# Fewer matmuls of ones at the start of an attention and gMLP kernel, and its first score tiles in the order of their loads

## The chip, the cores and the metric

The kernel runs on one core of one Trainium2 chip. The metric is device time in microseconds (us). Before the change three runs gave a median of 536.39 us (536.26 to 537.36).

The core has five engines that matter here: PE (TensorE, matmuls; its weight loads are listed as PEld), DVE (VectorE), ACT (ScalarE), POOL (GpSimd) and SP (SyncE, which issues the DMAs). Each runs its own list of instructions in order and waits for the others through semaphores.

## The reference

What is computed, for a batch of 8, 8 heads, 576 positions and a head dimension of 64:

```python
# sliding-window attention with a distance bias
scores = scale * np.matmul(q, k.transpose(0, 1, 3, 2))      # scale = 1/8
bias   = slopes[:, None, None] * (-np.abs(rel))             # rel = query position - key position
mask   = (rel >= 0) & (rel < 128)
scores = np.where(mask, scores + bias, -1e9)
attn   = softmax(scores)                                    # row max off, exp, divided by sum + 1e-9
x      = (attn @ v) as [batch, 576, 512]

# gated MLP with a spatial product
h      = np.maximum(x @ w_in, 0)                            # 512 -> 1024
u, v   = h[..., :512], h[..., 512:]
v_n    = (v - mean(v)) / sqrt(var(v) + 1e-6)
v_s    = einsum('ts,bsd->btd', w_spatial, v_n) + b_spatial
out    = (u * v_s) @ w_out
```

## The kernel before

**Work.** Eight batch entries go through the same chain: scores, softmax, the product with v, then units of the gated MLP called v, u, s (spatial) and o (output). Entry 0 is done in another way from entries 1 to 7. Its matmuls run on f32 operands, because the weights split into f16 halves aren't ready yet. It is cut into tiles: tile `tT P` is 128 query positions (two blocks of 64) of head pair P, for T = 0 to 4 and P = 0 to 3. Tile 0 needs only the first 128 columns of q and k; tile 1 needs columns 0 to 255.

**A tile of entry 0**, in the names of the code and of the rows below:
- `raw_tile` (letter t): PE writes two score blocks into two of four PSUM buffers s0 to s3 (L696). DVE adds the bias table, and takes the row extreme (L705). ACT takes the exponential, with the row sum (L709). Block widths are 64 and 128 columns for tile 0 and 192 for the others.
- `raw_sums` (letter m), once for each T: DVE adds 1e-9 and takes the reciprocal (L717, L718) once the four pairs of that tile row have their sums.
- `raw_out` (letter n): DVE or ACT scales the blocks (L730, L731), PE transposes them (L738, `ident`), DVE or ACT copies the transposed blocks to `pq` (L412), PE multiplies with v (L753), and DVE or ACT copies the result to `xt` (L412).

Beside these tiles DVE and ACT turn the weights, which arrive as 64-bit words, into f32 (`bits64`, L430 to L449, five steps over 128x512 for each of twelve pieces), and scale and split them.

**What sets the order.** Every piece of work is recorded in a `Plan` with its engine, an assumed weight in ns, a due time and the buffers that it reads and writes. Where `either` is used, the piece may go to ACT or to DVE. The string `OPENING` gives the order in which the opening's pieces are recorded, which fixes the turns on rotating buffers. `Plan.emit` then simulates the engines forward and backward up to 12 times on the assumed weights, takes the order whose simulated end is earliest, and writes each engine's list in that order. So a change in the string, or in one weight, reorders all engines. In that simulation PE's weights count double before `COLD`, and the DMAs cost more before `SLOW`.

**Matmuls of ones.** `constants` records `WARM` matmuls of a 128x256 block of ones into a PSUM buffer that nobody reads (L395). They depend only on the memsets, and the plan places them where it thinks that PE is free. `emit` has a second such device: where the plan shows PE idle for more than `SPARE` = 400 ns between `SLOW` = 9000 and `UNTIL` = 95000 ns of simulated time, it puts matmuls of ones of 128x128 into half of the rest of that gap (`filler`). In the kernel before, no gap calls for one.

**Loads.** SP issues the DMAs in the order of the plan. For entry 0 each head pair's q and k come in three pieces: 128, 256 and 192 columns (128, 256 and 192 KB).

Of the kernel before, what the change touches and what calls it, by code (L numbers as in the profile page):

```python
# [55 lines left out]
class Plan:  # L56
# [3 lines left out]

    PASSES, COLD, SLOW = 12, 6000, 9000
    LAG = {"PE": 200, "DVE": 130, "ACT": 130, "POOL": 150, "SP": 2200}

    def __init__(self):
# [125 lines left out]
                self.filler(int((idle - self.SPARE) * self.FILL / self.filler_ns))  # L192
            self.ops[n][0][best[2][n]][2]()

    SPARE, FILL, UNTIL = 400, 0.5, 95000

    def idle(self, out, way, ended, begun):

        last = None
        for n in out:  # L200
            gap = 0
            if self.ops[n][0][way[n]][0] == "PE":
                if last is not None and self.SLOW < begun[n] < self.UNTIL and begun[n] - ended[last] > self.SPARE:
                    gap = begun[n] - ended[last]
                last = n
            yield n, gap
# [3 lines left out]
def attn_gmlp_kernel(ctx, tc, qk, v, w_in, w_spT, b_sp, w_out, outT):  # L210
# [3 lines left out]
    nc = tc.nc  # L214
# [14 lines left out]
    NB = S // D  # L229

    SWITCH = 190
    SCORES, VALUES, BOTH = 1600, 1800, 2760


    WX = 12
    OPENING = (
# [8 lines left out]
    )  # L245
    UORDER = {B - 1: "uuuuusussusussssoooooooo"}
    USUAL = "uuuuusussususoooosssoooo"
# [32 lines left out]
    def pe(*cols):  # L280
        return sum(12 + n / 2.38 for n in cols)
# [114 lines left out]
            plan.add("PE", pe(2 * P), 0, f, [(ones, 0), (fill, 0)])  # L396

    SLOTS = 7
    WARM = 64
    NM_, SM_, TM_, RC_ = range(4)  # L400
    RSTAT = [(rstat, (i, k, c)) for i in range(2) for k in range(4) for c in range(2 * NP)]

# [280 lines left out]
    def raw_tile(p, t, k, raw, due):  # L683

        blocks = [i for i in (2 * t, 2 * t + 1) if i < NB]
        sc = [plan.buf(ps, "s", 4, [P, 512], F32) for _ in range(2)]
        flat = lambda e: sc[e]().rearrange("p a b -> p (a b)")
        st = lambda kind, e: rstat()[:, t % 2, kind, e * NP + p:e * NP + p + 1]
        key = lambda kind, e: (rstat, (t % 2, kind, e * NP + p))

        def f():
            for e, i in enumerate(blocks):
                n = min(i + 1, 3) * D
                for j in range(2):
                    q = slice((j ^ e) * D, ((j ^ e) + 1) * D)
                    nc.tensor.matmul(flat(e)[q, :n], raw()[j * D:(j + 1) * D, 0, i * D:(i + 1) * D],  # L696
                                     raw()[j * D:(j + 1) * D, 1, (i + 1) * D - n:(i + 1) * D], start=True, stop=True, skip_group_check=True)
        plan.add("PE", SWITCH + pe(4 * W), due, f, [(raw, x) for x in range(max(0, t - 1), t + 1)], [(x, 0) for x in sc])
        for e, i in enumerate(blocks):
            n = min(i + 1, 3) * D  # L700
            pr = lambda e=e, n=n: slot_ap(k)[:, W - n:W] if e == 0 else slot_ap(k)[:, 512 - n:]
            cols = slot_parts(k, e)

            def f(e=e, n=n, pr=pr):
                nc.vector.tensor_tensor_reduce(pr(), flat(e)[:, :n], tabs()[:, 2 * p + e, W - n:], -0.125, 3e38, ALU.add, ALU.min, st(NM_, e))  # L705
            plan.add("DVE", dve(n), due + 300, f, [(sc[e], 0), (tabs, 2 * p + e)], cols + [key(NM_, e)])

            def f(e=e, pr=pr):
                nc.scalar.activation(pr(), pr(), AF.Exp, bias=st(NM_, e), scale=-1.0, accum_out=st(SM_, e))  # L709
            plan.add("ACT", act(n, 2), due + 600, f, cols + [key(NM_, e)], cols + [key(SM_, e)])  # L710
# [10 lines left out]
    def raw_out(p, t, k, vr, xt, due):  # L721
# [2 lines left out]
        tiles = [x for x in (t - 1, t) if x >= 0]  # L724
        st = lambda e: rstat()[:, t % 2, RC_, e * NP + p:e * NP + p + 1]
        cols = [x for e in range(len(blocks)) for x in slot_parts(k, e)]
        for e, i in enumerate(blocks):
            n = min(i + 1, 3) * D
            pr = lambda e=e, n=n: slot_ap(k)[:, W - n:W] if e == 0 else slot_ap(k)[:, 512 - n:]
            plan.either([("ACT", act(n, 1), lambda e=e, pr=pr: nc.scalar.activation(pr(), pr(), AF.Copy, scale=st(e))),  # L730
# [15 lines left out]
        def f():  # L746
            for j in range(2):
                for n, x in enumerate(tiles):
                    c = n * P + j * D
                    ap = pf(c, c + D)  # L750
                    if len(blocks) == 2:
                        ap = bass.AP(ap.tensor, ap.offset, [ap.ap[0], [len(tiles) * P + D - 2 * j * D, 2], [1, D]])
                    nc.tensor.matmul(xp()[j * D:(j + 1) * D, :m], vr()[:, x, j * D:(j + 1) * D], ap,  # L753
                                     start=(n == 0), stop=(n == len(tiles) - 1), skip_group_check=True)
        plan.add("PE", SWITCH // 2 + 40 + pe(*[4 * m] * len(tiles)), due + 800, f, pcols + [(vr, x) for x in tiles], [(xp, 0)])
        qs = slice(t * P, t * P + m)
        copy(m, lambda: (xt()[:, qs], xp()[:, :m]), due + 1000, [(xp, 0)], xcols(xt, 0, qs.start, qs.stop))

    def clear():
# [364 lines left out]
    def record(kind, b, p):  # L1124
# [21 lines left out]
        elif kind == "t":  # L1146
            raw_tile(p, b, slot, loaded[0, p], at + p * 1000)
        elif kind == "m":
            raw_sums(b, at + 4900)
        elif kind == "n":  # L1150
            raw_out(p, b, slot, vraw[0, p], outs[0][p], at + 5000 + p * 500)
        elif kind == "L":
# [95 lines left out]
```

## Time and profile before

| | us |
|---|---|
| median of 3 runs (range) | 536.39 (536.26 to 537.36) |
| the profiled execution | 536.13 |
| its span, first to last instruction | 534.3 |
| busy in the span: PE, DVE, ACT | 525.6, 440.4, 409.8 |
| busy in the first 10 us: PE, DVE, ACT | 9.00, 6.28, 6.56 |

The profile is of one execution. A share of busy time is an average over stages: for PE it counts matmuls of ones as work. So the stages are read one by one from a view that cuts the span into stretches, and the waits from the view that says for each instruction how long its engine stood idle before it and who ended that.

### The profile page before, as it was taken

The numbers are of one execution on the slowest core, as the hardware profiler recorded it, in microseconds if no ns is written. First come the engines' busy times: TensorE is split into PE (matmuls) and PEld (weight loads), VectorE is DVE, ScalarE is ACT, GpSimd is POOL, SyncE is SP. The second block draws the span as 40 slices with busy tenths as digits, with TensorE's granted clock in tenths as the row PEclk, the third lists the DMA queues.
The fourth block names the chain that finished last, engine by engine and source line by source line (L and its number), as shares of the span: only waits on it lengthen the run. The fifth ranks groups of instructions, "written<-read, shape, count | busy, mean of one in ns | idle before, by whom it ended". The sixth has DMA issues, their size and how long they took to land.

```text
span 534.3 us, 15992 instructions
## 1 busy us (share of the span) xinstructions
PE 525.6 (98%) x6120; PEld 380.3 (71%) x6120; DVE 440.4 (82%) x1643; ACT 409.8 (77%) x1290; POOL 29.1 (5%) x75
## 2 busy tenths in 40 slices
PE   9999999999999999999999999999999999999997
PEld 5656567776687668885788758886688768774775
DVE  7999999999997887989999899988998898625440
ACT  7999999979986775969889778777976777534322
POOL 0000020001100010001100010001100010001000
PEclk9999999999999999999999999999999999999999
DMA  7987663978586533697769766766185435410002
GB/s 242 358 299 259 165 110 66 232 181 169 113 173 132 130 69 92 148 228 162 140 143 206 162 139 101 178 162 119 41 151 145 110 58 71 82 56 22 1 2 90
DMA packets 127665, 73.56 MB, mean 138 GB/s; under 512 B 105954, under 2 KB 118242, under 8 KB 127588
## 3 DMA queue, kind: packets, MB, share of 16 engines
q1 hardware_dynamic: 127588, 72.54, 57.5%
q8 instruction: 48, 0.79, 0.6%
q14 instruction: 29, 0.24, 0.2%
HBM read 37.13 MB, written 9.44 MB: 87 GB/s over the span
## 4 chain that ended last, share of the span: by engine, by line
PE 51%; DVE 3%; ACT 1%; issue 0%; POOL 0%; ACTq 0%; POOLq 0%
PE m L1058 13%; PE m L1098 11%; PE m L1037 11%; PE m L974 8%; PE x L896 3%; PE s L794 3%; PE m L1003 1%; DVE pq L848 1%; DVE st L932 0%; DVE prob L808 0%; ACT pq L843 0%; DVE vt L945 0%; DVE vn L985 0%; ACT prob L814 0%; DVE st L937 0%
## 5 line engine op out<-in xcount | busy, mean ns | idle before, releaser
L1058 PE MATMUL m<-wsp,vn 128*128 128x288 f16 x768 | 110.9, 286 | 0.0
L814 ACT ACTIVATE prob<-prob,stat 128x192 f32<-128x192 f32 (+2 forms) x252 | 107.0, 431 | 3.1 <-DVE stat L808 2.8
L843 ACT ACTIVATE pq<-prob,stat 128x192 f16<-128x192 f32 (+2 forms) x252 | 90.5, 428 | 5.7 <-DVE stat L837 1.9
L1058 PEld LDWEIGHTS <-vn 128*128 128x128 f16 x768 | 74.8, 98 | 19.6 <-issue 0.2
L848 DVE SCALAR_TENSOR_TENSOR pq<-prob,stat,pq 128x192 f16<-128x192 f32 (+2 forms) x252 | 87.3, 389 | 1.8 <-ACT pq L843 1.6
L1037 PE MATMUL m<-xt,win 128*128 128x288 f16 x672 | 87.9, 286 | 0.4 <-ACT vt L416 0.4
L1098 PE MATMUL m<-gs,wout 128*128 128x288 f16 x636 | 81.3, 286 | 0.0
L1037 PEld LDWEIGHTS <-win 128*128 128x128 f16 x672 | 65.2, 98 | 19.2 <-issue 1.3
L1098 PEld LDWEIGHTS <-wout 128*128 128x128 f16 x672 | 64.8, 98 | 16.5
L974 PE MATMUL m<-win,xt 128*128 128x512 f16 x336 | 75.5, 379 | 0.2 <-ACT o L1104 0.2
L808 DVE CUSTOM_DVE_ANT_0 prob<-s,tabs 128x192 f32<-128x192 f32 (+2 forms) x252 | 70.4, 329 | 5.4 <-PE s L794 5.3
L974 PEld LDWEIGHTS <-xt 128*128 128x128 f16 x336 | 32.2, 98 | 38.5 <-issue 2.4
L814 ACT ACTIVATION_READ_ACCUMULATOR prob<-prob,stat 128x1 f32 x252 | 49.2, 195 | 0.0
L1074 ACT ACTIVATE gs<-u 128x288 f16<-128x288 f32 x45 | 19.8, 440 | 36.4 <-DVE u L1071 36.3
L1071 DVE SCALAR_TENSOR_TENSOR u<-m,u 128x288 f32<-128x288 f32 x56 | 25.5, 455 | 22.1 <-PE m L1058 21.2
L794 PE MATMUL s<-qkraw 64*64 64x192 f32 (+1 forms) x1008 | 43.4, 310 | 0.0
L896 PEld LDWEIGHTS <-vh 64*64 64x64 f16 x1232 | 34.7, 106 | 10.5 <-issue 8.2
L896 PE MATMUL x<-pt,vh 64*64 64x192 f16 (+2 forms) x1232 | 39.6, 224 | 1.6 <-POOL am L905 1.6
L932 DVE BATCH_NORM_STATS2 st<-vt 128x6 f32<-128x512 f32 (+1 forms) x40 | 27.5, 689 | 12.4 <-ACT vt L416 12.0
L794 PEld LDWEIGHTS s<-qkraw 64*64 64x64 f32 x1008 | 36.3, 133 | 1.9 <-issue 1.6
L941 POOL TENSOR_TENSOR st<-st,nhalf 128x1 f32<-128x1 f32 (+1 forms) x40 | 25.4, 634 | 210.8 <-DVE st L937 179.7
L917 ACT ACTIVATE xt<-x 128x320 f16<-128x320 f32 (+1 forms) x56 | 19.9, 403 | 17.5 <-PE x L896 17.4
(181 smaller groups left out, 793.4 us busy)
## 6 DMA issues: line engine op xcount, KB each, us to landing
qkraw<-in_qk_dram SPq DMA_DIRECT2D x28, 576.0 KB, 4.9
out_dram<-o SPq DMA_DIRECT2D x64, 144.0 KB, 2.2
vraw<-in_v_dram SPq DMA_DIRECT2D x16, 320.0 KB, 3.8
wraw<-in_v_dram SPq DMA_DIRECT2D x12, 320.0 KB, 3.2
vn<-in_w_in_dram SPq DMA_DIRECT2D x4, 512.0 KB, 7.7
wout<-in_w_in_dram SPq DMA_DIRECT2D x4, 512.0 KB, 7.6
wout<-in_w_out_dram SPq DMA_DIRECT2D x4, 512.0 KB, 4.9
wraw<-in_w_spT_dram SPq DMA_DIRECT2D x4, 288.0 KB, 6.2
```

Of the source, the lines that this page charges most:

```text
L794: nc.tensor.matmul(flat(bank)[rows, c0:c0 + n], raw()[j * D:(j + 1) * D, 0, i * D:(i + 1) * D], raw()[j * D:(j + 1) * D, 1, (i + 1) * D - ...
L808: nc.vector.tensor_tensor_reduce(pt(), flat(bank)[:, c0:c0 + n], tabs()[:, 2 * p + odd, W - n:], -0.125, 3e38, ALU.add, ALU.min, st()[:, N ...
L814: nc.scalar.activation(pt(), pt(), AF.Exp, bias=st()[:, NM, k:k + 1], scale=-1.0, accum_out=st()[:, SM, k:k + 1])
L843: nc.scalar.activation(pq()[:, qc:qc + n], prob()[:, pc:pc + n], AF.Copy, scale=st()[:, RC, k:k + 1])
L848: nc.vector.scalar_tensor_tensor(pq()[:, qc + PLANE:qc + PLANE + n], prob()[:, pc:pc + n], st()[:, RC, k:k + 1], pq()[:, qc:qc + n], ALU.m ...
L896: done.append(nc.tensor.matmul(xps[half]()[j * D:(j + 1) * D, x0:x0 + len(ks) * D], l()[rows, kb // 2, j * D:(j + 1) * D], ap, start=(half ...
L932: nc.vector.bn_stats(st()[:m, 0:6], vt()[:m])
L974: nc.tensor.matmul(pt(), xt[c]()[:, a, t * P:(t + 1) * P], w[1, c]()[:, k, :], start=(n == 0), stop=(n == 3 * NC_ - 1))
L1037: nc.tensor.matmul(pt()[:, :HS], w[0, c]()[:, k, d * P:(d + 1) * P], xt[c]()[:, a, hf * HS:(hf + 1) * HS], start=(n == 0), stop=(n == 3 * ...
L1058: nc.tensor.matmul(pt()[:, :HS], l, r, start=(n == 0), stop=(n == len(ops) - 1))
L1071: nc.vector.scalar_tensor_tensor(u(), pt()[:, :HS], GATE * FINE, u(), ALU.mult, ALU.mult)
L1098: nc.tensor.matmul(pt()[:, :HS], wout[d]()[:, w, e * P:(e + 1) * P], gs[d]()[:, a, :], start=(n == 0), stop=(n == 3 * ND - 1))
```

## The change

- `WARM` goes from 64 to 13.
- The fillers may start at 3500 ns of simulated time (`FROM`) and no longer at 9000 (`SLOW`).
- `COLD` goes from 6000 to 5000, and the assumed weight `BOTH` of a products-with-scores turn of PE from 2760 to 2660.
- `OPENING` is another order of the same pieces. It begins with tile 1 of pair 0 (t10), then t01 of pair 1 and its tile 1.
- Code for tiles with T < `EARLY` is added, with `EARLY` = 0, so none of it is used.

```diff
-    PASSES, COLD, SLOW = 12, 6000, 9000
+    PASSES, COLD, SLOW = 12, 5000, 9000
...
-    SPARE, FILL, UNTIL = 400, 0.5, 95000
+    SPARE, FILL, FROM, UNTIL = 400, 0.5, 3500, 95000
...
-                if last is not None and self.SLOW < begun[n] < self.UNTIL and begun[n] - ended[last] > self.SPARE:
+                if last is not None and self.FROM < begun[n] < self.UNTIL and begun[n] - ended[last] > self.SPARE:
...
-    SCORES, VALUES, BOTH = 1600, 1800, 2760
+    SCORES, VALUES, BOTH = 1600, 1800, 2660
...
     OPENING = (
-        "t00 t02 t03 a03 t11 t01 t10 m00 n00 a00 n01 t13 w00 n02 t20 t12 t21 m10 n03 n11 n10 t22 n12 t23 w01 m20 n22 n13 w02 "
+        "t10 a03 t01 t11 Y00 t00 t03 t02 w00 m00 n00 t13 n01 t20 X03 t12 m10 n02 X00 t21 n03 w01 n11 a00 n10 t22 X02 n12 t23 "
...
-    WARM = 64
+    WARM = 13
+    EARLY = 0
```

SP's list at the very start, before. `qkraw_120`, `_129`, `_138` and `pt_145` are the buffers of the four head pairs' q and k, `vn3` receives a piece of the weights, and the last figures are partitions x 2 x columns:

```order
L639 DMA qkraw_120<-in_qk_dram 128x2x128
L639 DMA qkraw_129<-in_qk_dram 128x2x128
L639 DMA qkraw_138<-in_qk_dram 128x2x128
L639 DMA pt_145<-in_qk_dram 128x2x128
L639 DMA qkraw_129<-in_qk_dram 128x2x256
L456 DMA vn3_161<-in_w_in_dram 128x1024
L639 DMA qkraw_120<-in_qk_dram 128x2x256
L639 DMA pt_145<-in_qk_dram 128x2x256
L639 DMA qkraw_138<-in_qk_dram 128x2x256
```

and now (`qkraw_120`, `_137`, `_159` and `pt_150` are the four pairs):

```order
L640 DMA qkraw_120<-in_qk_dram 128x2x128
L640 DMA qkraw_120<-in_qk_dram 128x2x256
L640 DMA qkraw_137<-in_qk_dram 128x2x128
L640 DMA qkraw_137<-in_qk_dram 128x2x256
L640 DMA pt_150<-in_qk_dram 128x2x128
L640 DMA qkraw_159<-in_qk_dram 128x2x128
L640 DMA pt_150<-in_qk_dram 128x2x256
L457 DMA vn3_173<-in_w_in_dram 128x1024
L640 DMA qkraw_159<-in_qk_dram 128x2x256
```

The second piece of the first two pairs has moved up to places 2 and 4, and the weights' first piece back from place 6 to 8.

PE's list from the last of its first matmuls of ones on, before (the first 20 stand ahead of this; `s0` to `s3` are the score buffers):

```order
L395 LDWEIGHTS ones_75
L395 MATMUL x0_70<-ones_75 128x256
L696 MATMUL s0_66<-qkraw_120 64x64 x2
L696 MATMUL s1_67<-qkraw_120 64x128 x2
L395 LDWEIGHTS ones_75
```

and now, from the last of the six fillers (L339) that follow the 13 matmuls of ones:

```order
L339 LDWEIGHTS ones_75
L339 MATMUL s3_69<-ones_75 128x128
L697 MATMUL s0_66<-qkraw_120 64x192 x2
L697 MATMUL s1_67<-qkraw_120 64x192 x2
L697 MATMUL s2_68<-qkraw_137 64x64 x2
L697 MATMUL s3_69<-qkraw_137 64x128 x2
L697 MATMUL s0_66<-qkraw_137 64x192 x2
L697 MATMUL s1_67<-qkraw_137 64x192 x2
L697 MATMUL s2_68<-qkraw_120 64x64 x2
L697 MATMUL s3_69<-qkraw_120 64x128 x2
```

Before, a tile of 64 and 128 columns came first and more ones behind it; now a tile 1 comes first, and eight score tiles stand in a row with no ones between them. Behind the eighth stand ten fillers, and after them the first transposes.

DVE's list around the first reciprocal of row sums, before (`wx` is a piece of the weights on its way to f32):

```order
L705 ISA prob_98,rstat_102<-s1_67,tabs_77 128x128
L705 ISA rstat_102 128x1
L437 TENSOR_SCALAR wx_225<-wx_225 128x512
L441 TENSOR_SCALAR wx_225<-wx_225 128x512
L445 SCALAR_TENSOR_TENSOR wx_225<-vn3_161,wx_225 128x512
L717 TENSOR_SCALAR rstat_102<-rstat_102 128x8
L718 RECIPROCAL rstat_102<-rstat_102 128x8
```

and now:

```order
L706 ISA prob_98,rstat_102<-s3_69,tabs_77 128x128
L706 ISA rstat_102 128x1
L724 TENSOR_SCALAR rstat_102<-rstat_102 128x8
L725 RECIPROCAL rstat_102<-rstat_102 128x8
L738 TENSOR_SCALAR prob_98<-prob_98,rstat_102 128x128 x2
L738 TENSOR_SCALAR pt_152<-pt_152,rstat_102 128x64
L434 TENSOR_SCALAR wx_248<-vn3_173 128x512
```

The work on the weights that stood ahead of the first sums now stands behind them, so nothing lies between the twelfth score block and L724, the new line of L717.

## Rows read from the trace of the kernel before

**Rows 1.** Windows: us, busy PE PEld DVE ACT POOL (count), PEclk, DMA share, GB/s.

```profile
0.00:10.00 10.00, 9.01 (x80) 5.97 (x81) 6.28 (x45) 6.56 (x20) 1.02 (x7) 1.00 0.67 208
30.00:40.00 10.00, 9.11 (x59) 4.66 (x60) 9.68 (x41) 9.93 (x33) 0.00 (x0) 1.00 0.89 318
120.00:130.00 10.00, 10.00 (x58) 5.49 (x56) 9.79 (x37) 10.00 (x32) 0.59 (x1) 1.00 0.80 175
300.00:340.00 40.00, 40.00 (x453) 28.29 (x451) 36.55 (x136) 33.83 (x110) 3.24 (x7) 1.00 0.59 128
```

**Rows 2.** PE timeline: start us, us, engine, line, op, tiles, count, [idle before <-releaser].

```profile
0.99 4.45 PE L395 MATMUL x<-ones 128*128 128x256 bf16 x20 [0.99 <-DVE halves L357]
5.37 0.71 PE L696 MATMUL s<-qkraw 64*64 64x64 f32 x8
6.00 0.98 PE L395 MATMUL x<-ones 128*128 128x256 bf16 x4
8.98 1.92 PE L395 MATMUL x<-ones 128*128 128x256 bf16 x16
...
34.46 3.70 PE L967 MATMUL m<-wx,xt 128*128 128x512 f32 x8
...
44.22 0.44 PE L738 MATMUL m<-ident,pt 128*128 128x128 f32 x2 [0.67 <-ACT pq L412]
```

**Rows 3.** DVE timeline to the first reciprocal.

```profile
2.89 1.92 DVE L390 TENSOR_SCALAR tabs<-u,halves 128x192 bf16<-128x192 f32 x8
5.89 0.23 DVE L705 CUSTOM_DVE_ANT_0 prob<-s,tabs 128x64 f32<-128x64 f32 x1 [1.09 <-PE s L696]
7.29 0.23 DVE L705 CUSTOM_DVE_ANT_0 prob<-s,tabs 128x64 f32<-128x64 f32 x1 [0.87 <-PE s L696]
8.86 0.36 DVE L705 CUSTOM_DVE_ANT_0 pt<-s,tabs 128x192 f32<-128x192 f32 x1 [0.77 <-PE s L696]
9.43 0.22 DVE L705 CUSTOM_DVE_ANT_0 prob<-s,tabs 128x64 f32<-128x64 f32 x1
9.78 0.42 DVE L437 TENSOR_SCALAR wx<-wx 128x512 f32<-128x512 f32 x1
11.31 0.16 DVE L717 TENSOR_SCALAR rstat<-rstat 128x8 f32<-128x8 f32 x1
```

**Rows 4.** ACT timeline, the same stretch.

```profile
3.45 0.62 ACT L386 COPY pt<-zero 128x512 f32<-128x512 f32 x1
6.16 0.35 ACT L709 ACTIVATE prob<-prob,rstat 128x64 f32<-128x64 f32 x1 [2.09 <-DVE rstat L705]
7.56 0.35 ACT L709 ACTIVATE prob<-prob,rstat 128x64 f32<-128x64 f32 x1 [0.57 <-DVE rstat L705]
11.81 1.17 ACT L730 ACTIVATE prob<-prob,rstat 128x64 f32<-128x64 f32 x4 [0.55 <-DVE rstat L718]
```

**Rows 5.** SP timeline, the first four loads.

```profile
0.74 2.00 SPq L639 DMA_DIRECT2D qkraw<-in_qk_dram  x3
2.78 0.61 SPq L639 DMA_DIRECT2D pt<-in_qk_dram  x1
```

**Rows 6.** DMA view, loads one and four: KB, us from issue to landing.

```profile
qkraw<-in_qk_dram SPq DMA_DIRECT2D x1, 128.0 KB, 2.6
pt<-in_qk_dram SPq DMA_DIRECT2D x1, 128.0 KB, 3.3
```

**Rows 7.** DMA view, 0 to 40 us in slices of 1 us.

```profile
GB/s 0 0 135 185 188 173 368 313 330 388 333 280 390 404 409 394 406 406 411 412 383 389 400 388 195 215 199 246 278 192 220 284 301 369 426 436 341 267 346 193
```

**Rows 8.** PE groups, first of 0 to 5.3 us, then of 8.9 to 10.8.

```profile
L395 PE MATMUL x<-ones 128*128 128x256 bf16 x20 | 4.4, 420 | 1.0 <-DVE halves L357 1.0
...
L395 PE MATMUL x<-ones 128*128 128x256 bf16 x16 | 1.9, 273 | 0.0
```

**Rows 9.** ACT groups, 5 to 60 us: busy us, mean ns | idle before.

```profile
L709 ACT ACTIVATE prob<-prob,rstat 128x192 f32<-128x192 f32 x11 | 4.9, 445 | 0.0
L709 ACT ACTIVATE prob<-prob,rstat 128x128 f32<-128x128 f32 x3 | 1.2, 388 | 0.0
L709 ACT ACTIVATE prob<-prob,rstat 128x64 f32<-128x64 f32 x3 | 1.0, 346 | 2.7 <-DVE rstat L705 2.7
```

More of the change, by code (lines that the diff above doesn't have):

```diff
@@ L706, in raw_tile, with f @@
             plan.add("DVE", dve(n), due + 300, f, [(sc[e], 0), (tabs, 2 * p + e)], cols + [key(NM_, e)])
+            if t < EARLY:
+                def f(e=e, pr=pr):
+                    nc.scalar.activation(pr(), pr(), AF.Exp, bias=st(NM_, e), scale=-1.0)
+                plan.add("ACT", act(n, 1), due + 600, f, cols + [key(NM_, e)], cols)
+                continue
             def f(e=e, pr=pr):
@@ L726, in raw_out @@
         cols = [x for e in range(len(blocks)) for x in slot_parts(k, e)]
-        for e, i in enumerate(blocks):
+        for e, i in enumerate(blocks if t >= EARLY else ()):
             n = min(i + 1, 3) * D
@@ L754, in f @@
                                      start=(n == 0), stop=(n == len(tiles) - 1), skip_group_check=True)
-        plan.add("PE", SWITCH // 2 + 40 + pe(*[4 * m] * len(tiles)), due + 800, f, pcols + [(vr, x) for x in tiles], [(xp, 0)])
-        qs = slice(t * P, t * P + m)
+                    if t < EARLY:
+                        nc.tensor.matmul(xp()[j * D:(j + 1) * D, 2 * P:2 * P + m], ones()[:, :D], ap, start=False, stop=(n == len(tiles) - 1),
+                                         skip_group_check=True)
+        plan.add("PE", SWITCH // 2 + 40 + pe(*[4 * m] * len(tiles)) * (2 if t < EARLY else 1), due + 800, f, pcols + [(vr, x) for x in tiles] + [(ones, 0)],
+                 [(xp, 0)])
+        qs = slice(t * P, t * P + m)
+        if t < EARLY:
+            sm = plan.buf(work, "sm", 2, [P, P], F32)
+            plan.add("ACT", act(m), due + 900, lambda: nc.scalar.activation(sm()[:, :m], xp()[:, 2 * P:2 * P + m], AF.Copy, bias=1e-9), [(xp, 0)], [(sm, 0)])
+            plan.add("DVE", 100 + dve(m), due + 950, lambda: nc.vector.reciprocal(sm()[:, :m], sm()[:, :m]), [(sm, 0)], [(sm, 0)])
+            plan.add("DVE", dve(m), due + 1000, lambda: nc.vector.tensor_tensor(xt()[:, qs], xp()[:, :m], sm()[:, :m], ALU.mult),
+                     [(xp, 0), (sm, 0)], xcols(xt, 0, qs.start, qs.stop))
+            return
         copy(m, lambda: (xt()[:, qs], xp()[:, :m]), due + 1000, [(xp, 0)], xcols(xt, 0, qs.start, qs.stop))
@@ L1148, in record @@
         elif kind == "m":
-            raw_sums(b, at + 4900)
+            if b >= EARLY:
+                raw_sums(b, at + 4900)
         elif kind == "n":
```

14 rows, old and new, of the table OPENING are left out of this document.

## The prediction

> **What bounds the kernel now.** I read the busy time by stretches first. From 120 us on PE is busy in every microsecond [rows 1], and its matmuls of ones are long over, so from there the end is PE's work and nothing else. That work is the same after the change. What the change can move is how late PE gets there. In the opening the other two engines set that: from 30 to 40 us DVE is busy 9.68 and ACT 9.93 of 10 us, while PE, with 9.11, still waits now and then [rows 1]. Only the first 10 us are slack: DVE 6.28, ACT 6.56.
>
> The timelines say where that slack lies. DVE is through with its constants at 2.89 + 1.92 = 4.81, waits 1.09 us for the first score tile, then 0.87 and 0.77 for the next ones: 2.73 us [rows 3]. ACT is through at 3.45 + 0.62 = 4.07 and waits 2.09, 0.57 and 0.55: 3.21 us [rows 4]. In all that time PE is "busy": with 20 matmuls of ones to 5.37, four more from 6.00, sixteen from 8.98 [rows 2]. So a busy PE hides two things there: loads that haven't landed, and ones that stand ahead of a score tile.
>
> The budget is therefore 2.73 us on DVE and 3.21 on ACT, before either is saturated. Nothing that the change does later can be read from an idle engine, since there is hardly one until 120 us.
>
> **Step 1: the first tile's start.** PE is free after 13 ones at 4.45 / 20 = 0.22 us each from 0.99, at 3.9 [rows 2], and after six fillers of half the width at 0.11, at 4.55. The first tile is now t10 and needs the first two loads, 128 + 256 KB = 0.39 MB. Loads one to four, 0.52 MB, have passed at 5.1 by the slices (135 + 185 + 188 KB to 5.0) [rows 7], and the fourth landed at 2.78 + 3.3 = 6.1 [rows 5, 6]: 1.0 us behind its last byte. The first landed at 0.74 + 2.6 = 3.3, with its 0.13 MB passed at 3.0: 0.35 behind. At the rate of the old first slices 0.39 MB have passed at 4.4; at the 368 GB/s of the slice in which wider pieces move, at 3.0 + 0.26 / 0.368 = 3.7. So the landing is between 4.05 and 5.4. I take 4.8, in the middle: the second load is of the wide kind, but issued 0.67 us behind the first. The fillers are hidden by that load; if it lands first, they cost 0.5 us at most.
>
> DVE began 0.52 behind the tile's start (5.37 to 5.89) [rows 2, 3]; with 192 columns I take 0.6, so 5.4. ACT began 0.27 behind DVE [rows 4]; a block of 192 is 0.14 longer on DVE (0.285 against 0.14, from the starts 8.86 and 9.43 below), so 0.4, and ACT begins at 5.8. ACT's idle time is then 5.8 - 4.07 = 1.7.
>
> **Step 2: the row of eight tiles.** From 8.86 to 9.43 DVE does two blocks of 192, 0.285 each; from 9.43 to 9.78 the two blocks of a first tile, 0.35 [rows 3]. The twelve blocks ahead of the first reciprocal are two tiles of the wide kind and four first tiles: 4 x 0.285 + 4 x 0.35 = 2.54 us, to 7.9 if each load is there. ACT needs for the eleven exponentials that the first reciprocal waits for 3 x 0.445 + 4 x 0.346 + 4 x 0.388 = 4.27 us [rows 9], so to 5.8 + 4.27 = 10.1. DVE has nothing else in its list and waits 2.1 us there, at L724. That is the new wait: it takes the place of the three waits for PE. DVE's idle time is 0.6 + 2.1 = 2.7, as before. ACT's is 1.7, since it runs without a break from 5.8, against 3.21. L724 comes at 10.1 instead of 11.31 [rows 3], but the weights' three steps that stood ahead of it are still to be done.
>
> The eighth tile needs the ninth load: 2.1 MB have passed at 10.05 by the old slices [rows 7]. Behind it stand ten fillers, 0.6 to 1.1 us by the two rates of ones, and then the transposes. The blocks that those wait for are scaled by ACT behind L724, from about 10.6 on, so this costs 0 to 0.5 us. I take 0, as DVE and ACT have other work in that time.
>
> **Step 3: what becomes of it.** 3.21 - 1.7 = 1.5 us on ACT and 0.0 on DVE. Scalings and copies can go to either engine, so the gain is shared: 0.75 us for both. It reaches PE in full: PE has ones to give up, and from there all three are tied together until PE is saturated. Bounds: 0.4 with the load at 5.4, 1.2 with the load at 4.05.
>
> **Step 4: the rest of the order.** The second and third v units of entry 0 now stand ahead of its first u unit. PE's wait of 0.67 us at 44.22 [rows 2] lies there, and a unit of 3.7 us, as at 34.46, could fill it. No row shows the new places. The bounds are that wait gained and, on the other side, as much lost by a like wait elsewhere; I take 0.2 gained, since the v units need work that is done early. The weight `BOTH` acts only through the order and goes with this.
>
> Sum: 0.75 + 0.2 = 0.95 us. The profiled execution took 536.13 around a span of 534.3, so it would come to a span of 533.35 and 535.2. The median of the runs is 0.26 above that execution: 535.4.
>
> **The matmul clock.** The column of granted clock says 1.00 from the first stretch on [rows 1], but the same matmul of ones takes 420 ns to 5.3 us and 273 ns from 8.9 on [rows 8], and starts every 0.22 us and then every 0.12 [rows 2]: that is the 1.2 GHz level, and then the 2.4 one. It rose after PE had worked without a gap from 0.99, some time after 6.0, where four ones still take 0.98. Removing 51 ones takes away just such work. The Trainium skill, page "TensorE: Matmul & The Clock Gate", section "What's actually happening", has the low rate as the default state, which activity releases. That speaks against this change: a PE that waits for loads and for DVE from 4.6 to 10 may stay low for longer. By that rule the result is rival D; the trace agrees that the start is at the low level, and has no stretch of the opening with PE waiting. If the level rises as before, the rule changes nothing.
>
> **Rivals.**
> A, the forecast, 535.4 (0.3 to 1.6 below before): 0.45. For it: the waits are measured and PE's ones are what stood there.
> B, more: DVE's wait at L724 isn't 2.1 us but is spread, and the waits behind 34 us go as well. Then ACT's 1.5 counts in full, and 0.67: 2.2 us, 534.2. For it: the plan shares work between the two engines; against it: DVE's list has nothing ahead of L724. 0.23.
> C, nothing: the gain of ACT is taken back, because from 12 to 24 us the loads come at some 400 GB/s without a break [rows 7] and so can't come earlier than they do; or because the reordering loses what step 1 gains. 536.3, 0.12. Against it: no row shows an engine waiting for a load there.
> D, slower: the clock stays at the low level through the first transposes. After 6.9 PE has 40 ones left, about 4.8 us of the 10.4 to 17.3, so 5.6 us of work. About 2.5 of it are score tiles, which have time until 10. The other 3.1 takes 6.2 at half the rate, with 18 fillers at 0.11 another 2.0, in the 5.9 us from 10.4 to 16.3, so PE is 2.3 us late and the engines behind it too; against the forecast 537.7. It decides from the point where the low level lasts past 13 us. For it: PE's list has waits from the fifth microsecond on. Against it: eight tiles and sixteen fillers keep PE at work for much of that time. 0.20.
>
> **How the numbers follow.** A measurement can tell about 0.2%, or 1.07 us, from no change, so below 535.3 counts as faster. A lies across that edge: of its 0.45, 0.20 fall below it, and 0.25 above. B is faster, C the same, D slower. Faster 0.43, same 0.37, slower 0.20. A alone runs from 534.8 to 536.1. The range takes in B and most of D: 533.7 to 537.6.
>
> **What would show it.** Right: the first score matmul between 4.5 and 5.4, no idle ACT of over 0.3 us from then to 10, one wait of DVE of about 2 us at L724 near 10.1, the first matmul of the v unit near 33.5 instead of 34.46. Step 1 is wrong if the first tile waits beyond 5.4. Step 2 is wrong if ACT waits between tiles for loads. D is right if transposes or score blocks behind 10 us show twice their old spacing. B is right if DVE's idle time up to 12 us comes out far under 2.7. The forecast is wrong as a whole if waits of PE appear between 35 and 120 us that before doesn't have.

## The result and the profile after

| | before | after |
|---|---|---|
| median (range), us | 536.33 (535.41 to 537.36), 22 runs | 538.67 (537.02 to 542.74), 22 runs |
| ratio to before, 95% interval | | 1.0054 (1.0039 to 1.007) |
| the profiled execution, its span | 536.13, 534.3 | 538.76, 536.7 |
| mean granted clock in the span | 1.00 | 0.994 |

The change made the kernel slower by 2.3 us; the forecast was 535.4, 1 us faster. The first stretch of the kernel after, in the columns of [rows 1], and the one from 60 to 70 us before and then after:

```profile
0.00:10.00 10.00, 6.61 (x71) 4.64 (x75) 6.71 (x48) 7.20 (x26) 1.02 (x7) 0.89 0.65 185
...
60.00:70.00 10.00, 10.00 (x32) 4.57 (x31) 9.79 (x45) 9.98 (x35) 1.12 (x2) 1.00 0.61 137
...
60.00:70.00 10.00, 7.70 (x62) 4.84 (x62) 8.06 (x32) 7.65 (x29) 0.00 (x0) 1.00 0.77 166
```

The first ten microseconds look as wished: DVE 6.71 and ACT 7.20 instead of 6.28 and 6.56. But the stretch from 60 to 70 us has a hole: PE, DVE and ACT are each idle for about 2 us where they had hardly any slack before. PE's list shows where. Its timeline, after, to be read against [rows 2]:

```profile
0.99 2.95 PE L395 MATMUL x<-ones 128*128 128x256 bf16 x13 [0.99 <-DVE halves L357]
3.74 0.81 PE L339 MATMUL s<-ones 128*128 128x128 bf16 x6
5.12 0.77 PE L697 MATMUL s<-qkraw 64*64 64x192 f32 x16 [0.58 <-DMA qkraw<-in_qk_dram]
...
9.89 0.92 PE L697 MATMUL s<-pt 64*64 64x192 f32 x8 [0.75 <-DMA pt<-in_qk_dram]
...
11.38 1.25 PE L339 MATMUL s<-ones 128*128 128x128 bf16 x10
12.42 1.79 PE L745 MATMUL m<-ident,prob 128*128 128x128 f32 x6
...
35.77 3.70 PE L985 MATMUL m<-wx,xt 128*128 128x512 f32 x8
...
66.16 1.94 PE L1015 MATMUL m<-wx,xt 128*64 128x512 f32 x8 [2.30 <-ACT u L417]
```

Three things are to be seen. The first tile starts at 5.12, 0.25 earlier than before. The first v unit, which has the same matmuls but for ones ahead of it in both kernels, starts at 35.77 instead of 34.46, 1.31 later. And at 66.16, ahead of the v unit for the last 64 positions (the remainder unit below), PE has waited 2.30 us for a copy of ACT. Before, the same unit started without a wait:

```profile
65.36 1.94 PE L997 MATMUL m<-wx,xt 128*64 128x512 f32 x8
```

DVE's waits in the opening (against [rows 3]) and its one long wait later:

```profile
5.70 0.36 DVE L706 CUSTOM_DVE_ANT_0 pt<-s,tabs 128x192 f32<-128x192 f32 x1 [0.89 <-PE s L697]
7.33 0.36 DVE L706 CUSTOM_DVE_ANT_0 pt<-s,tabs 128x192 f32<-128x192 f32 x1 [0.62 <-PE s L697]
8.76 0.29 DVE L706 CUSTOM_DVE_ANT_0 pt<-s,tabs 128x128 f32<-128x128 f32 x1 [0.27 <-PE s L697]
10.45 0.17 DVE L724 TENSOR_SCALAR rstat<-rstat 128x8 f32<-128x8 f32 x1 [0.96 <-ACT prob L716]
12.88 0.36 DVE L706 CUSTOM_DVE_ANT_0 prob<-s,tabs 128x192 f32<-128x192 f32 x1 [0.54 <-PE m L745]
15.16 0.36 DVE L706 CUSTOM_DVE_ANT_0 pt<-s,tabs 128x192 f32<-128x192 f32 x1 [0.41 <-PE s L697]
...
65.85 0.16 DVE L480 TENSOR_REDUCE vsc<-vsc 128x1 f32<-128x4 f32 x1 [1.87 <-ACT vt L473]
```

And ACT's, against [rows 4]:

```profile
6.10 0.46 ACT L716 ACTIVATE pt<-pt,rstat 128x192 f32<-128x192 f32 x1 [2.04 <-DVE rstat L706]
...
13.10 0.80 ACT L413 COPY pq<-m 128x256 f32<-128x256 f32 x2 [0.72 <-PE m L745]
...
64.99 0.74 ACT L473 ACTIVATE vt<-vraw 128x640 bf16<-128x640 f32 x1 [2.35 <-DMA vraw<-in_v_dram]
...
65.72 0.39 ACT L417 ACTIVATE u<-m 128x288 f32<-128x288 f32 x1
```

The last two rows are the 2.3 us. ACT's list has a row limit of a piece of v for entry 1 (L473), and behind it the u copy that PE waits for. The piece had not landed, so ACT stood for 2.35 us, the copy with it, and PE behind the copy. Why it had not landed is in SP's list: after, then before.

```profile
51.46 4.64 SPq L653 DMA_DIRECT2D vraw<-in_v_dram  x2
...
57.52 1.15 SPq L640 DMA_DIRECT2D qkraw<-in_qk_dram  x1
58.76 0.38 SPq L653 DMA_DIRECT2D vraw<-in_v_dram  x1
```

```profile
45.10 0.33 SPq L652 DMA_DIRECT2D vraw<-in_v_dram  x1
...
46.83 3.31 SPq L652 DMA_DIRECT2D vraw<-in_v_dram  x2
```

The pieces of v for entry 1 are four. They turn through four buffers (`vraw`) with three pieces of entry 0's v, so the first finds a buffer free and leaves SP early in both kernels (28.68 us before, 30.45 after). Each of the other three needs a buffer that comes free when PE has done tile 4's product with v (L753 before, L760 now). Before, they left between 45.10 and 50.1 us; after, the first of the three leaves at 51.46 and the last at 58.76. The new order puts v unit 2 of entry 0 ahead of those products and v unit 3 behind the first of them, so they run from 50.95 to 57.8 us where before had them from 44.6 to 49.3. The waits of SP between 40 and 62 us, after (us in total, times, longest):

```profile
SPq L653 <- PE x L760: 9.0, 2, 5.1
SPq L640 <- PE s L812: 1.7, 1, 1.7
```

SP waits for the products in its own order, and the last piece stands behind a q/k load (L640) that in turn waits for scores.

PE's work from 40 to 140 us, before and then after:

```profile
40.00:140.00 100.00, 98.14 (x1025) 66.50 (x1022) 97.09 (x357) 95.13 (x295) 6.09 (x13) 1.00 0.73 170
...
40.00:140.00 100.00, 96.29 (x1029) 66.64 (x1030) 96.19 (x356) 93.22 (x303) 6.51 (x12) 1.00 0.71 174
```

The sum of the profile: from 40 to 140 us PE is idle 3.71 us of 100 (before 1.86), from 140 to 300 us 0.69 of 160 (before 0.53), and as much as before later. That makes 1.85 + 0.16 = 2.0 of the 2.4 us by which the span is longer; the other 0.4 us is lost up to 40 us.

### The profile page after: what moved, and what is told of

The parts are those of the page before. It is cut to its first block, busy times and chain, and to the rows that moved or that the text cites. A ratio compares the mean times of both kernels' runs of the same rounds, so it can differ in the third digit from the quotient of the medians.

```text
span 536.7 us, 15942 instructions
## 1 busy us (share of the span) xinstructions
PE 522.9 (97%) x6091; PEld 379.5 (71%) x6093; DVE 439.6 (82%) x1639; ACT 411.3 (77%) x1296; POOL 30.3 (6%) x75
## 4 chain that ended last, share of the span: by engine, by line
PE 90%; DMA 6%; ACT 1%; SPq 1%; DVE 1%; issue 0%; POOL 0%; POOLq 0%; ACTq 0%
PE m L1076 20%; PE m L1055 16%; PE m L1116 15%; PE m L992 14%; PE s L812 7%; PE x L914 6%; PE m L1108 3%; DMA vraw<-in_v_dram 2%; PE m L985 2%; PE m L1047 2%; DMA qkraw<-in_qk_dram 2%; PE m L1021 2%; DMA vn<-in_w_in_dram 2%; SPq L640 1%; PE x L760 1%; PE m L745 1%
## 5 line engine op out<-in xcount | busy, mean ns | idle before, releaser
L861 ACT ACTIVATE pq<-prob,stat 128x192 f16<-128x192 f32 (+2 forms) x252 | 89.2, 429 | 2.1 <-ACT u L417 1.4
L914 PEld LDWEIGHTS <-vh 64*64 64x64 f16 x1232 | 34.7, 106 | 10.8 <-issue 8.1
L959 POOL TENSOR_TENSOR st<-st,nhalf 128x1 f32<-128x1 f32 (+1 forms) x40 | 26.5, 663 | 218.8 <-DVE st L955 202.1
L950 DVE BATCH_NORM_STATS2 st<-vt 128x6 f32<-128x512 f32 (+1 forms) x40 | 27.5, 688 | 10.8 <-ACT vt L417 10.3
```

The source lines that it names most:

```text
L861: nc.scalar.activation(pq()[:, qc:qc + n], prob()[:, pc:pc + n], AF.Copy, scale=st()[:, RC, k:k + 1])
L914: done.append(nc.tensor.matmul(xps[half]()[j * D:(j + 1) * D, x0:x0 + len(ks) * D], l()[rows, kb // 2, j * D:(j + 1) * D], ap, start=(half ...
L950: nc.vector.bn_stats(st()[:m, 0:6], vt()[:m])
L959: nc.gpsimd.tensor_tensor(st()[:m, 11:12], st()[:m, 10:11], nhalf()[:m], ALU.pow)
```

## The experiments

In each, "held" means that every instruction stays in the order that the planner gave the kernel from which the experiment starts; "planned anew" means that the planner made another order. The kernel before took 536.08, 535.95, 535.95 and 536.01 us in the four batches. The marks of all profiles, in us (the mark "v unit" is its first matmul, "idle" is PE's idle time of the 100 us from 40 to 140):

| kernel | order | ratio (95%) | v unit | idle |
|---|---|---|---|---|
| before | | | 34.46 | 1.86 |
| after | | 1.0054 (1.0039 to 1.007) | 35.77 | 3.71 |
| e2_vbuf | after, held but one load | 1.0005 (0.9996 to 1.0014) | 35.72 | 1.42 |
| f2_bufonly | after, held | 1.002 (1.0008 to 1.0033) | 35.09 | 1.38 |
| h1_before6real | before, held | 1.0001 (0.9992 to 1.0009) | 34.89 | 2.25 |
| f1_limitlater | after, seven moved | 1.008 (1.0066 to 1.0094) | 35.45 | 4.72 |
| f5_past_copies | after, few moved | 1.0035 (1.0022 to 1.0048) | 35.34 | 2.94 |
| e1_ones | after, held | 1.0034 (1.0023 to 1.0045) | 35.47 | 3.00 |
| e3_both | as e2 | 1.0006 (0.9996 to 1.0016) | 35.52 | 1.50 |
| e4_before13 | before, held | 1.0017 (1.0009 to 1.0026) | 34.27 | 1.86 |
| p1_ahead13 | before, held | 1.0 (0.9991 to 1.0009) | 34.17 | 2.01 |
| g2_before6 | planned anew | 1.0012 (1.0003 to 1.002) | 35.40 | 2.30 |
| p3_ones | planned anew | 1.0024 (1.0015 to 1.0033) | 35.58 | 2.73 |
| p2_costs | planned anew | 1.0028 (1.0017 to 1.0039) | 35.24 | 3.13 |
| f4_newopening | planned anew | 1.0029 (1.0018 to 1.004) | 35.75 | 1.92 |
| p4_tiles | planned anew | 1.0034 (1.0021 to 1.0046) | 35.14 | 2.27 |
| f3_oldopening | planned anew | 1.0051 (1.0037 to 1.0065) | 36.64 | 2.68 |
| g1_after6 | planned anew | 1.006 (1.0048 to 1.0072) | 35.03 | 3.10 |

**The late loads.** Theory: the wait for the load makes the loss. Rival: the low matmul clock of the opening makes it.

e2_vbuf gives the kernel after six real buffers for the pieces of v, and issues the last piece ahead of the q/k load:

```diff
+    REAL = {"vraw": 6}
+        real = self.REAL.get(tag, bufs)
+    # in emit: the load ("L", 2, 0) goes behind the load ("D", 1, 3)
+            rows.insert(z, rows.pop(a))
```

> The changed kernel in its own order, but entry 1's v goes to buffers of its own where there is room (six in place of four), and its last piece is issued ahead of the q and k load it stood behind. Theory late loads: SP waits 5 us for a product with v to free a buffer, the last piece of v lands at 64.9, ACT's row limit for it stands ahead of two copies that PE needs, and PE loses 2.3 us at the remainder's v unit. Then that wait falls under 0.5 us and the median falls by 1.5 to 2.3 us, to about 536.7; the clock's low stretch and the spread stay. Rival displaced: DVE and ACT are the limit there anyway, so the wait only moves on and the time changes by less than 0.5 us.

Measured 536.36 us (535.49 to 538.0), 2.3 below the kernel after and no different from before. SP's list and PE's unit in it:

```profile
46.49 1.62 SPq L670 DMA_DIRECT2D vraw<-in_v_dram  x2
...
57.58 1.16 SPq L670 DMA_DIRECT2D vraw<-in_v_dram  x1
58.84 0.38 SPq L657 DMA_DIRECT2D qkraw<-in_qk_dram  x1
```

```profile
63.86 1.94 PE L1032 MATMUL m<-wx,xt 128*64 128x512 f32 x8
```

Two pieces leave 5 us earlier, the last 1.2 us earlier, and the remainder unit, which started at 66.16 behind a wait of 2.30, starts at 63.86 behind none. So the late loads, at the place where ACT's list needs them, make the loss. f2_bufonly has the buffers without the swap:

```diff
+    REAL = {"vraw": 6}
```

> The changed kernel in its own order with six buffers for the big v pieces instead of four, and nothing else. The load of the third piece then waits for no product of tile 4 but still stands behind a q/k load whose buffer the scores release. Theory (the buffers are what made the load late): the two first loads of entry 1 leave SP 5 us earlier, the third is out by 58.0 instead of 58.8, ScalarE's wait for it falls from 2.35 to under 1.6 us, and the time is 537.0 to 537.8. Rival (the place behind the q/k load alone decides): nothing changes, 538.3 to 538.9. Second rival (buffers alone decide): 536.2 to 536.6, as with both.

537.12 us (535.85 to 538.78): by the medians 1.55 below the kernel after and 0.8 above e2. The last piece left at 57.48, ACT waited 0.33 us for it, PE 0.28. So the buffers make most of the gain. The control is the same six buffers in the order of before:

```diff
+    REAL = {"vraw": 6}    # in the kernel before
```

> The kernel before in its own order, with six buffers for the big v pieces instead of four: the control for the two runs with buffers. Theory (buffers cure a stall that only the new order has): 535.7 to 536.3, no change. Rival (buffers help any order, so those runs say nothing of the change): 534.0 to 535.2.

536.21 us: nothing. The buffers cure a stall that only the new order has.

**Is it ACT's line or the load?** f1_limitlater moves the row limit and what hangs on it far down, behind the copies:

```diff
+        moved = [limit, at[("G", 1, 0), "DVE"][0], at[("G", 1, 0), "SP"][0]]
+        return [x for k, x in enumerate(rows[:use]) if k not in moved] + take + rows[use:]
```

> The changed kernel, every instruction on every engine in its order but for seven: ScalarE's row limit and cast of the third big v piece of entry 1 (the one that waited 2.35 us for its load), with the reduction, cast and transpose that hang on it, stand some nine ScalarE instructions later, behind the two u copies that TensorE waits for. Theory (a load that comes late stops ScalarE in its order, and with it the copies behind): TensorE's wait of 2.3 us at the remainder of the v unit is gone or under 0.5 us, and the time falls by 1.0 to 2.2 us, to 536.4 to 537.6. Rival (the late piece itself is what the next stage needs): the wait comes back a few us later, at the reduction or the transpose, and the time stays at 538.2 to 539.0.

540.17 us (539.83 to 540.6), 1.5 more. The rival holds, and more: PE's remainder unit starts at 63.60 without a wait, but 13 us later:

```profile
76.51 0.36 PE L927 MATMUL x<-pt,vh 64*64 64x192 f16 x8 [2.00 <-DVE vh L896]
```

The limit now ran at 68.37, 3.4 us later than in the kernel after, too far to be a fair test. f5_past_copies moves it three ACT instructions only:

```diff
+        past = act[act.index(limit) + 3]
+        moved = [limit, *(k for k in range(limit, past) if self.labels[rows[k][0]] == ("G", 1, 0))]
```

> The changed kernel; the late piece's row limit moves only three ScalarE instructions down, just behind the two u copies, with its reduction, cast and transpose behind it; everything else in its order, four buffers. It starts then at the same 65.0 us as before the move. Theory (the head of ScalarE's line is the loss): TensorE's 2.3 us wait goes and does not come back, 536.4 to 537.4. Rival (the chain from the late load over the limit, the reduction and the transpose to entry 1's product is late itself, and only shows at the copies): a wait of 1 to 2.5 us appears at that product (L927's place, near 75 us), and the time is 538.0 to 539.0.

538.15 us (537.22 to 539.19): 0.5 less than the kernel after by the medians, 1.0 by the ratios, whose intervals overlap. The time lies in the rival's range, but the wait came at other places than the rival had it. ACT's wait, then DVE's, then PE's:

```profile
65.37 0.74 ACT L483 ACTIVATE vt<-vraw 128x640 bf16<-128x640 f32 x1 [1.29 <-DMA vraw<-in_v_dram]
```

```profile
66.23 0.16 DVE L490 TENSOR_REDUCE vsc<-vsc 128x1 f32<-128x4 f32 x1 [2.22 <-ACT vt L483]
```

```profile
67.26 0.87 PE L822 MATMUL s<-qkraw 64*64 64x192 f32 x16 [0.64 <-DVE stat L836]
70.98 3.70 PE L995 MATMUL m<-wx,xt 128*128 128x512 f32 x8 [0.71 <-DVE vt L1038]
```

PE no longer waits for ACT. DVE now stands for the late piece in its own list (the reduction over the row limits), and PE waits 0.64 + 0.71 us for the DVE instructions behind that. Here the late load stopped the list in which its consumer stood, and moving the consumer moved the stall.

The same late loads need not cost this. f4_newopening (below, the new string alone, planned anew) sends the three pieces at 51.69, 54.14 and 58.30, as late as the kernel after. But in its order ACT does the limit of the last piece at 66.81, behind the copies of u, and PE's remainder unit doesn't wait:

```profile
58.30 0.33 SPq L652 DMA_DIRECT2D vraw<-in_v_dram  x1
```

```profile
64.45 1.94 PE L997 MATMUL m<-wx,xt 128*64 128x512 f32 x8
```

So the stall is the late load together with the place of its consumer in ACT's list.

**The ones and the clock.** Theory: of the 64 ones the 7 that stood between the thirteenth and the first tile were in the way. Rival: the ones keep the clock up, and taking them away costs.

p1_ahead13 leaves out just those 7 in the order of before; the other 44 stay between the tiles:

```diff
-        for _ in range(WARM):
-            def f():
+        for k in range(WARM):
+            def f(k=k):
+                if 13 <= k < 20:
+                    return
```

> The kernel before in its order with 13 instead of 20 ones ahead of the first score tile, the other 44 where they stand between the tiles. If the first tile starts when its load has landed (5.32 us where nothing stood ahead): first tile at 5.2 to 5.4, time unchanged, 535.6 to 536.3. If the ones were in the way, as the prediction had it: first tile at 4.5 to 4.9 and 535.0 to 535.5. If 13 ones ahead leave the matmul clock low for longer: 536.4 to 537.1.

```profile
3.87 0.71 PE L698 MATMUL s<-qkraw 64*64 64x64 f32 x8
...
5.44 0.45 PE L698 MATMUL s<-qkraw 64*64 64x64 f32 x8
6.62 0.45 PE L698 MATMUL s<-pt 64*64 64x64 f32 x8 [0.74 <-DMA pt<-in_qk_dram]
...
34.17 3.70 PE L969 MATMUL m<-wx,xt 128*128 128x512 f32 x8
```

536.25 us, ratio 1.0. The first tile started 1.50 us earlier (3.87 instead of 5.37), so the ones did stand ahead of a landed load. The expectation was wrong to give 5.32 as the time of the first tile: in e4 (next) that is the second one. But the third tile had to wait for its load until 6.62, the v unit came 0.29 earlier, and the time gained nothing. In this order an earlier first tile is worth nothing, because PE waits for the next loads.

e4_before13 leaves out all 51 in the order of before:

```diff
+                if k >= 13:
+                    return
```

> The kernel before in its own order, with only the first 13 of its 64 ones issued. Theory clock: with PE idle between the tiles the clock falls or rises late in some executions: stretches granted 0.50 or the slow spacing after 7 us, the median 1 to 2.5 us above the kernel before, the spread over 3 us. Rival: the ones were only in the way of score tiles, so the first tile starts at about 4 instead of 5.4 and the time falls by up to 1 us, with the spread of before (2 us).

537.05 us (535.74 to 537.87). Against p1, the 44 ones between the tiles are worth 0.9 us (1.0017 against 1.0). The trace shows how PE works without them; the last row is one of before, for comparison:

```profile
3.87 0.71 PE L698 MATMUL s<-qkraw 64*64 64x64 f32 x8
5.32 0.70 PE L698 MATMUL s<-qkraw 64*64 64x64 f32 x8 [0.74 <-DMA qkraw<-in_qk_dram]
...
12.45 0.92 PE L698 MATMUL s<-qkraw 64*64 64x192 f32 x8
```

```profile
12.87 0.56 PE L696 MATMUL s<-qkraw 64*64 64x192 f32 x8
```

Before, eight such matmuls of 192 columns take 0.56 us at 12.87; here they still take 0.92 at 12.45, although the granted clock of that microsecond reads 1.00. The profiled execution (535.74) is the fastest of the 11, though, and its v unit, at 34.27, is not late: so it does not show where the median's 1 us goes. The clock of all executions tells a part: five of the 11 have a mean granted clock of 0.987 to 0.990 over the span, and their median is 537.34; the other six, at 0.999 or more, have 536.92, still 0.7 above p1. The rest stays open.

e1_ones puts 43 more ones between the first eight tiles of the kernel after:

```diff
+            if self.labels[n] and self.labels[n][0] == "t" and self.ops[n][0][0][0] == "PE":
+                self.filler(self.MORE.pop(0) if self.MORE else 0)
+    MORE = [3, 2, 10, 4, 6, 4, 8, 6]
```

> The changed kernel in its own order, with 43 more matmuls of ones (128x128) put between its eight first score tiles, where PE waits. Theory clock: what costs time in the opening is the low level of the matmul clock from 7.9 to 14.6 us, which comes because PE stands idle between the tiles. Then no stretch after the first rise is granted 0.50, the first matmul of a v unit (35.77 in the changed kernel, 34.46 before) comes by 34.6, the median falls by 1 to 1.5 us to about 537.3 and the runs spread over less than 2.5 us (5.7 in the changed kernel). The wait of 2.3 us at the remainder's v unit stays. Rival order: the loads and DVE's wait for the exponentials set the opening, and ones only add work: the v unit comes at 35.8 or later, the time is the same or up to 2 us longer.

537.71 us (536.62 to 540.19), 1.0 below the kernel after; the spread is 3.6 us, not under 2.5. In the profile the stretch of lower granted clock (below) is gone and PE's wait at the remainder unit is 1.5 instead of 2.3 (the last piece of v leaves SP at 57.93 instead of 58.76), but the v unit comes only 0.30 earlier. e3_both has e1's and e2's edits together:

```diff
+    REAL = {"vraw": 6}
+    MORE = [3, 2, 10, 4, 6, 4, 8, 6]
```

> Both edits at once, the more ones between the score tiles and the earlier loads of v. If both theories hold and their places are independent, the two gains add: 3 us or more below the changed kernel, 535.2 and so about 1 us below the kernel before, with a spread under 2.5 us. If only one holds, the time is that of the one alone. If the opening's order is itself worse, it stays above 536.3.

536.34 us, as e2 has without the ones (536.36). The two gains don't add: with the loads in time, the ones, and the clock with them, are worth nothing in this order.

**Which part of the change?** f3_oldopening has all of the change but the string; f4_newopening only the string; p2_costs only `COLD` and `BOTH`; p3_ones only `WARM` and `FROM`; p4_tiles only the order of t, m and n in the string; g1_after6 and g2_before6 tell the planner of six `vraw` buffers, in the kernel after and before. All are planned anew.

```diff
-        "t10 a03 t01 t11 Y00 t00 t03 t02 w00 m00 n00 t13 n01 ...   # f3; f4 the other way round
+        "t00 t02 t03 a03 t11 t01 t10 m00 n00 a00 n01 t13 w00 ...
-        "t00 t02 t03 a03 t11 t01 t10 m00 n00 a00 n01 t13 w00 ...   # p4
+        "t10 t01 t11 a03 t00 t03 t02 m00 n00 a00 t13 n01 w00 ...
-    PASSES, COLD, SLOW = 12, 6000, 9000    # p2
+    PASSES, COLD, SLOW = 12, 5000, 9000
-    SCORES, VALUES, BOTH = 1600, 1800, 2760
+    SCORES, VALUES, BOTH = 1600, 1800, 2660
-    WARM = 64                              # p3
+    WARM = 13
-    SPARE, FILL, UNTIL = 400, 0.5, 95000
+    SPARE, FILL, FROM, UNTIL = 400, 0.5, 3500, 95000
-            vr = plan.buf(work, *(("vraw", NP) ...   # g1, g2
+            vr = plan.buf(work, *(("vraw", 6) ...
```

f3:

> The changed kernel with the string of the first order (which ranks the opening operations) put back to that of before; thirteen ones, fillers from 3.5 us on, and the planner's two changed costs stay. Theory (the new order, not the ones, costs the 2.3 us): no wait of TensorE for a u copy at 66 us, 536.2 to 537.2, the upper end where the clock falls as it did when the old order had thirteen ones (537.05). Rival (ones and costs make the loss): 538.0 to 538.9.

f4:

> The kernel before with only the new string of the first order; 64 ones, the old costs and fillers. Theory (the new order costs it): the v units of entry 0 stand ahead of tile 4's products with v, the loads of entry 1 are late, TensorE waits 1.5 to 2.5 us between 60 and 70 us, 537.4 to 538.6. Rival (the loss needs ones and order together, for instance through the clock): 536.0 to 536.8.

g1:

> The changed kernel with six buffers for the big v pieces, known to the planner, so that the order is planned anew. If the new order's stall came from the four buffers alone: 535.5 to 536.6. If any order that is planned anew gets a stall of its own somewhere before 140 us, as the last two did: 537.0 to 538.5, with 1 to 2 us more idle TensorE between 40 and 140 us than the 1.86 of before.

g2:

> The kernel before with six buffers known to the planner: old string, old costs, 64 ones, a new plan. If a plan made anew costs something by itself: 536.6 to 538.0. If only the change's own numbers cost: 535.5 to 536.2.

p2:

> The kernel before with only the planner's two numbers changed (end of doubled costs 5 instead of 6 us, 2660 instead of 2760 ns for a unit of products), planned anew. If these numbers make the new order's loss: 537.5 to 538.8. If any new plan costs something by chance: anywhere from 536.2 to 539. If neither: 535.6 to 536.2.

p3:

> The kernel before with thirteen ones and fillers from 3.5 us on, old string and old costs, planned anew. If few ones make the loss (low clock over the first 15 us): 537.0 to 537.6, as where 13 ones stood in the held order (537.05). If the new plan adds a stall of its own: 537.6 to 539. If the ones cost nothing: 535.6 to 536.3.

p4:

> The kernel before with only its raw tiles, sums and outputs (t, m, n) in the new string's order, everything else of the old string in its place, 64 ones, old costs, planned anew. If the new tile order starves VectorE (it starts with two tiles of 192 columns; in the run with the new string its first 20 us held 14.9 us of work instead of 16.1): VectorE's first 20 us hold 15.0 to 15.5 us, the first v unit comes 0.6 to 1.2 us later, 536.5 to 537.3. If tile order costs nothing: 535.6 to 536.3.

Measured: f3 538.47, f4 537.27, g1 539.55, g2 536.61, p2 537.43, p3 537.29, p4 537.79 us. The theory that the new string alone makes the loss fell with f3: the old string with the rest of the change loses as much. It missed in f4 too, where the wait of 1.5 to 2.5 us between 60 and 70 us doesn't appear. Each part alone makes a slower kernel: the string by 1.3 us, the two costs by 1.4, the ones with their fillers by 1.3, the order of the tiles by 1.8. And g2, which has nothing of the change, is 0.7 slower, though its buffers in the held order cost nothing (h1). What these seven have in common is the new plan. In each the v unit is 0.6 to 2.2 us later than before, and in each PE is idle longer between 40 and 140 us, in f4 hardly (1.92) but in its place 1.39 of the 160 us from 140 to 300. The waits differ: in p2 the longest of PE are 1.0 and 0.8 us for copies of ACT, in p4 1.5 for a step of the weights on DVE. In none of the seven was the cause taken away by itself, so that the new plan is the cause is argued and not shown. For p3 a rival stands: its time lies in the range that its expectation gave to few ones, and e4, with as many ones in the held order, lost 1.1 us. p4's expectation was that the wide tiles starve DVE; its first 20 us hold 15.99 us of DVE's work against 16.14, so that was not it.

No version beat the kernel before; p1, h1, e2 and e3 equal it.

## Why the prediction was wrong

**Step 1 (first tile's start): right, a little short.** The tile started at 5.12 (forecast 4.8, bounds 4.05 to 5.4), DVE at 5.70 (5.4), ACT at 6.10 (5.8). ACT's first idle time is 2.04 us instead of the 3.21 of [rows 4]; 1.7 was forecast.

**Step 2 (the row of eight tiles): right up to the first reciprocal.** DVE's idle time to there is 0.89 + 0.62 + 0.27 + 0.96 = 2.74, forecast 2.7, though it is spread and not one wait of 2.1. The reciprocal's L724 came at 10.45 (forecast 10.1, before 11.31), and ACT ran without a break from 6.10 to 12.4. The step took 0 for the ninth load and the ten fillers. The load that cost PE 0.75, at 9.89, was the seventh (the second piece of `pt`, for tile t13); the fillers took 1.25 at 11.38, and the transposes came at 12.42, no earlier than before. For them ACT waited 0.72 at 13.10 and DVE 0.54 at 12.88; DVE's 0.41 at 15.16 was for score matmuls behind them.

**Step 3 failed: the gain did not reach PE "in full".** The windows from 0 to the first v unit, before and after, show what became of it:

```profile
0.00:34.46 34.46, 32.44 (x337) 20.44 (x337) 30.29 (x146) 30.40 (x104) 1.02 (x7) 1.00 0.87 296
```

```profile
0.00:35.77 35.77, 30.12 (x309) 19.47 (x309) 30.32 (x146) 31.95 (x110) 1.02 (x7) 0.90 0.84 279
```

ACT is idle for 4.06 us before (34.46 - 30.40) and 3.82 after: of the 1.17 it gained at the start only 0.24 was left. And it does 1.55 us more work ahead of the v unit (110 instructions instead of 104), where DVE does the same 30.3. The copies are most of it, before and then after, by groups from 0 to 36 us:

```profile
L412 ACT COPY pq<-m 128x512 f32<-128x512 f32 (+1 forms) x7 | 3.8, 541 | 0.0
```

```profile
L413 ACT COPY pq<-m 128x512 f32<-128x512 f32 (+1 forms) x10 | 4.9, 495 | 0.8 <-PE m L745 0.7
```

"The gain is shared" was assumed of a plan that instead gave ACT more. This is read from one trace of each kernel; no run moved the copies back. The v unit was forecast at 33.5 and came at 35.77; in the sum of the span, a gain of 0.75 was a loss of 0.4. A late v unit is not the whole loss: e2 has it at 35.72 and takes no longer than before. p1 adds that the gain would not have come in the old order either. (The step's upper bound of 1.2 also leaves out the six fillers that step 1 lets run to 4.55; with them it would be 0.9.)

**Step 4 failed, and it is the main error.** It bounded "the rest of the order" by 0.67 us on either side, from a wait that the trace of before happens to show, and wrote that no row shows the new places. The order did show the v units moved ahead. Not followed was what they were moved past: tile 4's products, whose end frees the buffers that SP waits for, for loads that ACT's list needs at 62 us. And not followed was where the late load's consumer stands: in front of the copy that PE needs (in f4, where it stands behind, the late loads make no wait there). The measured wait is 2.30 us, over three times the bound, and taking it away gave 2.3 us back. The gain that the step hoped for was real: with the loads in time (e2) PE is idle 1.42 us between 40 and 140, 0.44 less than before.

**Rivals.** D came closest (537.7) and its mechanism is in the trace. The granted clock after, in stretches of a microsecond:

```profile
7.00:8.00 1.00, 0.77 (x20) 0.53 (x12) 0.68 (x5) 1.00 (x5) 0.00 (x0) 0.89 0.68 201
8.00:9.00 1.00, 1.00 (x16) 0.74 (x14) 0.73 (x9) 1.00 (x7) 0.00 (x0) 0.50 0.89 309
...
13.00:14.00 1.00, 0.96 (x5) 0.43 (x4) 1.00 (x7) 0.85 (x3) 0.00 (x0) 0.50 1.03 384
14.00:15.00 1.00, 1.00 (x15) 0.64 (x18) 0.76 (x4) 1.00 (x6) 0.00 (x0) 0.69 1.06 408
```

After waits of 0.58 and 0.85 us for a load and for DVE the clock fell to 0.50 (the 1.2 GHz level) and stayed there to between 14 and 15; D had put its point of decision at 13. By the Trainium skill, page "TensorE: Matmul & The Clock Gate", section "What's actually happening", the low rate is the default state, which activity releases; these rows agree.

What the fall costs depends on the loads. With the late loads in place it goes with a longer time: of the 22 executions of the kernel after, the nine with a mean granted clock of 0.999 or more over the span have a median of 537.44 us, the 13 with 0.997 or less 540.18. With the loads in time it doesn't: e2's six executions at 0.999 or more have 536.2, its six at 0.997 or less 536.4, and e3 gains nothing over e2. So D is a part of the loss and not its root: without the fall 1.1 us is still lost (537.44 against 536.33), e1 took back only 1.0, and e2 took back 2.3 with the fall still in its trace. By what path the fall adds to the late loads was not traced.

A, B and C had no row for a stall behind 40 us; the last sentence of the prediction, that waits of PE between 35 and 120 us would make the forecast wrong as a whole, is what happened. (PE is not quite busy in every microsecond from 120 us on, as the prediction has it: before, it is idle 0.53 us from 140 to 300 and 0.55 from 300 to 500.)

## What to carry to other kernels

When a planner sets the order, price the places to which work moves, not the work: follow each moved unit past every instruction it overtakes, and ask whose buffers those free, which load, in which queue, waits for them, and what stands behind that load's consumer. A new plan may be a change by itself: seven of seven were 0.7 to 3.6 us slower here, one of them with nothing of the change in it. So test an idea in the held order first (p1 would have shown that the earlier first tile is worth nothing). And an engine's slack at the start is worth only what is not lost again before the next stage.

## What was not expected

- The first load of q and k (128 KB, issued at 0.74) is there by 3.87 at the latest; the next tile, which needs the second load or a later one, started at 4.97 (p3) to 5.32 (e4) where PE waited for it.
- What matmuls that nobody reads are worth depends on the order: 44 of them 0.9 us in the old one (e4 against p1); in the new one 43 of half the width took back 1.0 us while the loads were late (e1), and nothing once they were in time (e3 against e2).
